# Packed bias operands, twelve early probability tiles through TensorE, bias tables scaled on three engines, two k magnitudes moved

## The chip, the cores and the metric

The kernel is one program on one core of a Trainium2 chip. A core has five engines that run at the same time, each with its own in-order list of instructions: TensorE (PE, matrix products and transposes, with its weight loads shown as PEld), VectorE (DVE), ScalarE (ACT), GpSimd (POOL) and SyncE (SP), which here issues every DMA. The metric is device time in microseconds from the start of the program to its end. Three unprofiled runs of the kernel before took 1791.48, 1793.86 and 1797.2 us; the median, 1793.86 us, is its time. The profile is of one more execution, which took 1798.62 us, with a span of 1796.5 us from the first to the last instruction.

## The reference

An attention layer over 4 batches, 8 heads, 576 positions and head size 64, with a learned additive bias that depends on the two positions only, followed by a layer of eight experts that all see all 2304 rows:

```python
scores = scale * np.matmul(q, k.transpose(0, 1, 3, 2))
x = (log1p(abs(rel)) / log1p(maximum(pos, 1)))[..., None]
h = np.maximum(x @ w1 + b1, 0.0)          # 32 hidden units
scores = scores + (h @ w2).transpose(2, 0, 1)[None]
attn = softmax(scores)
out = np.matmul(attn, v)                  # becomes x of the experts, 2304 x 512
P = exp(x @ w_gate - max), then 8 rounds of row and column normalisation
for e in range(8):
    out += P[:, e:e+1] * (np.maximum(x @ w1[e], 0.0) @ w2[e])
```

## The kernel before

Every operand of a matrix product is split into two fp16 parts, `hi` and `lo`, and three products are added in place of one.

**The order of the work.** In the first part (attention, and the start of expert 0) the Python code does not issue instructions. It records them as nodes with a guessed cost, and `Plan.emit` sorts them: it walks through a modelled time and puts on each engine what is ready first. The order on each engine's list is therefore an outcome of the guessed costs, and any change in the nodes moves other instructions too. All nodes go through one helper line, L202 in the profile, so instructions are told apart by their tiles.

**The bias (blocks 0 to 40).** A host table `xm` holds operands for the 32 hidden units. `bias_front(i)` takes one block `x` of it, loaded by `xm_load` into the tile `xmt` (which lies in `area`), multiplies it by the weights `wa` on PE (into `pv` and the `l` banks) and takes the sign on ACT into `sg` (also in `area`). `bias_back(i)` multiplies the signs by a table on PE (into `s`) and combines the result on DVE. For query tiles 0 and 1 the bias stays on chip in the tables `br[0]` and `br[1]`; tiles 2 and 3 go through a staging tile to `sc_bias` in DRAM and come back per head pair as `bt`; the half tile 4 is kept in `br4`.

**The scale of q and k.** The largest magnitudes of q and k are needed before any score. Sixteen pieces of 128 x 1152 are loaded, q pieces reduced on DVE (`TENSOR_REDUCE`) and k pieces on ACT (`Abs` with a running sum, `some_max`). From them come `mqk`, a broadcast over PE, the scale `s_qk`, and the factor `gbox[0]` by which the tables `br` are then multiplied (`b_scale`, one call per head pair `hp`, two operations each). The same is done for eight pieces of v (`v_max`), which sit in the buffers `bt` and `aT`.

**Attention.** There are 16 units (a batch and a pair of heads), each of 5 steps: two steps of two query tiles for each of the two tile groups `gi` 0 and 1 (one per head `hh`), and one step for the half tile (`gi` 2). Steps 0 to 7 are the `gi` 0 steps of units 0 to 3, run together with the bias blocks; steps 8 to 19 are the `gi` 1 and `gi` 2 steps of these units; after that each unit runs its five. One step is: scores on PE into one of two `s` buffers, bias and maximum on DVE (`sb`), exponential on ACT, `hi` part on ACT and `lo` part on DVE into `ah` (two buffers), a DMA that transposes `ah` into `aT`, and the product with v on PE (`pv`), two steps later.

**Expert 0.** Once the bias blocks have freed `area`, its weights are loaded there (`area<-in_moe_w_dram`), their magnitudes taken, and cut into `hi` and `lo` on ACT and DVE (`w_cut`, the 128 x 1024 operations on `area`). From step 15 on pieces of expert 0 (`l<-xa,area` and the like) are put between the steps on PE. The rest of expert 0 and experts 1 to 7 follow when attention is over.

Of the kernel before, what the change touches and what calls it, by code (L numbers as in the profile page):

```python
# [9 lines left out]
F16 = mybir.dt.float16  # L10
# [3 lines left out]
ALU = mybir.AluOpType  # L14
# [9 lines left out]
N = B * S  # L24
NT = N // P
R = S // 64
EPS = 1e-9
T14 = 2.0**14
TM14 = 2.0**-14
# [233 lines left out]
def attention_sinkhorn_moe(ctx, tc, q, k, v, w1, b1, w2, wg, m1, m2, xm, xm4, xf, sel, out):  # L263
# [141 lines left out]
    with ExitStack() as actx:  # L405
# [64 lines left out]
        def xm_load(i):  # L470
            if i >= NBLK:
                return
            t, s0, n = blk(i)
            x = hidp.tile([P, 4, P], F16, name="xmt", tag="xm", bufs=4)[:, : n // 16, :]
            src = (xm[t] if t < 4 else xm4).rearrange("p (m i) -> p m i", i=P)
            sync.dma_start(out=x, in_=src[:, s0 // 16 : (s0 + n) // 16, :])
            xq[i] = x
# [57 lines left out]
        def bias_front(i):  # L535
            t, s0, n = blk(i)
            W = 8 * n
            xm_load(i + 3)
            if i % 9 == 3 and t < 4:
                xg_load(t + 1)  # L540
            x = xq.pop(i)
            sg = hidp.tile([P, 4, 512], F16, name="sg", tag="sg")
            for g4 in range(4):
                pre = ps_l1() if g4 % 2 else psA.tile([P, 512], F32, name="pre", tag=("pv", "l2")[g4 // 2])
                pe.matmul(pre[:, :W], wa[:, g4], x, start=True, stop=True)
                act.activation(sg[:, g4, :W], pre[:, :W], AF.Sign)
            sgs[i] = sg

# [238 lines left out]
        for n in range(8):  # L787
            for m in (2 * n, 2 * n + 1):
                nm, _, i = qk_order[m]
                some_max(mq8[:, int(nm == "k"), i : i + 1], mxt.pop((nm, i)), nm == "k")  # L790
                if m + 4 < 16:
                    max_load(*qk_order[m + 4])
                elif m + 4 == 16:
                    u_load(0)
                if m + 4 >= 16:
                    max_load("v", v, m - 12)
            bias_step()
            bias_step()
# [20 lines left out]
        def b_scale(hp):  # L819

            for t in range(2):
                x = br[t][:, 2 * hp : 2 * hp + 2, :]
                vec.tensor_scalar(out=x, in0=x, scalar1=gbox[0], scalar2=None, op0=ALU.mult)


        mv8, vbox = sm([P, 8]), []
# [128 lines left out]
        def st_lo(s):  # L955
            n, ah = len(s["sb"]), s["ah"]
            s["aT"] = wrk.tile([P, 9 * n, P], F16, name="aT", tag="aT" if n == 2 else "aT4", bufs=3 if n == 2 else 1)
            for i, sb in enumerate(s["sb"]):
                vec.scalar_tensor_tensor(
                    out=ah[:, i, S:],  # L960
                    in0=sb,
                    scalar=s["st"][:, 3, i : i + 1],
                    in1=ah[:, i, 0:S],
                    op0=ALU.mult,
                    op1=ALU.subtract,
                )
            sync.dma_start_transpose(out=s["aT"], in_=ah.rearrange("p n s -> p (n s)"))

        def attend(u, gi, ss):

# [922 lines left out]
def _constants():  # L1893
    import numpy as np

    pos = np.arange(S)
    rel = (pos[:, None] - pos[None, :]).astype(np.float32)
    x = np.log1p(np.abs(rel)) / np.log1p(np.maximum(pos[:, None].astype(np.float32), np.float32(1.0)))
    x = x.astype(np.float32)
    x4 = x * np.float32(4.0)  # L1900
    hi = x4.astype(np.float16)
    lo = (x4 - hi.astype(np.float32)).astype(np.float16)
    p = np.arange(64)
    half = lambda r: 9 * p + r
    key = np.concatenate([half(c + 4 * r) for c in range(4) for r in range(2)] + [half(8)])
    tiles = [np.concatenate([half(t), half(t + 4)]) for t in range(4)] + [half(8)]
    res, xf = [], []
    for tk in tiles:
        xr = x[np.ix_(tk, key)]
        if len(tk) == P:  # L1910
            xf.append(xr)
        else:
            half_keys = np.concatenate([xr[:, : S // 2], xr[:, S // 2 :]])
            xf.append(np.concatenate([half_keys, 0 * half_keys], axis=1))
        a = np.zeros((4, 32, 36, len(tk)), np.float16)
        for part, src in enumerate((hi, hi, lo, lo)):
            g = src[np.ix_(tk, key)].reshape(len(tk), 36, 4, 4)
            if len(tk) < P:
                g = g.reshape(len(tk), 2, 18, 4, 4).transpose(0, 2, 1, 3, 4).reshape(len(tk), 36, 4, 4)
            a[:, 4 * part : 4 * part + 4] = g.transpose(2, 3, 1, 0)  # L1920
        a[:, 16:18] = 4.0
        res.append(a.reshape(128, -1))
    sel = np.zeros((4, 32, 24), np.float32)
    for g in range(4):
        for r in range(18):
            sel[g, r, r // 4 % 2 if r < 16 else r - 14] = 1.0
            sel[g, r, 8 + 4 * g + np.arange(4)] = [float(r >= 16 or r % 4 == j) for j in range(4)]
        sel[g, :, 4 + g] = 1.0
    return np.stack(res[:4]), res[4], np.stack(xf), sel.reshape(128, 24)


# [26 lines left out]
```

## Time and profile before

| what | value |
|---|---|
| median of three runs | 1793.86 us (1791.48 to 1797.2) |
| profiled execution | 1798.62 us, span 1796.5 us |
| PE busy | 1686.3 us, 94% of the span |
| DVE busy | 1445.9 us, 80% |
| ACT busy | 1086.0 us, 60% |
| POOL busy | 78.7 us, 4% |
| mean granted TensorE clock | 0.979 of full speed |

The shares are means over very different stretches. Attention and the bias fill about the first 530 us; the experts, in which PE is hardly ever idle, fill the rest. The change touches the first 280 us or so, and those have to be read by stretches.

### The profile page before, as it was taken

The numbers are of one execution on the slowest core, as the hardware profiler recorded it, in microseconds if no ns is written. First come the engines' busy times: TensorE is split into PE (matmuls) and PEld (weight loads), VectorE is DVE, ScalarE is ACT, GpSimd is POOL, SyncE is SP. The second block draws the span as 40 slices with busy tenths as digits, with TensorE's granted clock in tenths as the row PEclk, the third lists the DMA queues.
The fourth block names the chain that finished last, engine by engine and source line by source line (L and its number), as shares of the span: only waits on it lengthen the run. The fifth ranks groups of instructions, "written<-read, shape, count | busy, mean of one in ns | idle before, by whom it ended". The sixth has DMA issues, their size and how long they took to land.

```text
span 1796.5 us, 40453 instructions
## 1 busy us (share of the span) xinstructions
PE 1686.3 (94%) x16640; PEld 1375.3 (77%) x16640; DVE 1445.9 (80%) x2627; ACT 1086.0 (60%) x1930; POOL 78.7 (4%) x90
## 2 busy tenths in 40 slices
PE   7787698898989999999999999999999999999998
PEld 4444365555566688888888898889888988898887
DVE  6897888888968798779787887878788878876666
ACT  7887787878856675545564555464555544453443
POOL 0120011222200000000000000000000000000000
PEclk9998699899999999999999999999999999999999
DMA  8879999999993354654475457345645653463321
GB/s 273 256 182 207 224 189 186 190 196 192 199 249 141 104 176 165 219 177 169 174 264 168 173 186 268 135 162 200 235 165 177 222 204 133 157 236 108 104 74 36
DMA packets 305817, 326.55 MB, mean 182 GB/s; under 512 B 191584, under 2 KB 234336, under 8 KB 300640
## 3 DMA queue, kind: packets, MB, share of 16 engines
q1 hardware_dynamic: 305632, 323.97, 60.8%
q8 instruction: 130, 2.13, 0.5%
q14 instruction: 55, 0.45, 0.1%
HBM read 192.18 MB, written 88.08 MB: 156 GB/s over the span
## 4 chain that ended last, share of the span: by engine, by line
PE 76%; DVE 9%; DMA 9%; ACT 3%; issue 2%; SPq 0%; POOL 0%; DVEq 0%; ACTq 0%; POOLq 0%
PE bankA L1581 18%; PE bankA L1601 13%; PE bankE L1601 9%; PE bankE L1581 9%; PE bankB L1601 8%; PE l L202 6%; PE bankB L1581 4%; DMA aT<-ah 4%; PE pv L202 4%; PE s L202 3%; DVE area L202 2%; DVE ah L202 1%; ACT area L202 1%; DVE sb L202 1%; DMA xc<-in_moe_w_dram 1%
## 5 line engine op out<-in xcount | busy, mean ns | idle before, releaser
L1581 PEld LDWEIGHTS <-slot 128*128 128x128 f16 x5040 | 450.7, 98 | 49.7 <-issue 3.8
L1601 PEld LDWEIGHTS <-hA 128*128 128x128 f16 x2268 | 221.8, 98 | 26.7 <-issue 0.6
L202 PEld LDWEIGHTS <-area 128*128 128x128 f16 x2477 | 153.0, 99 | 108.4 <-issue 39.8
L1581 PE MATMUL bankA<-xt,slot 128*128 128x256 f16 (+1 forms) x1680 | 186.1, 262 | 1.6 <-ACT u L1638 1.6
L1581 PE MATMUL bankE<-xt,slot 128*128 128x256 f16 (+1 forms) x1680 | 186.1, 262 | 0.0
L1626 ACT ACTIVATE hA<-c 128x512 f16<-128x512 f32 x189 | 118.1, 627 | 111.0 <-DVE c L1204 110.1
L1601 PEld LDWEIGHTS <-hS 128*128 128x128 f16 x1512 | 147.1, 98 | 23.4 <-ACT hS L1626 3.4
L1601 PEld LDWEIGHTS <-area 128*128 128x128 f16 x1512 | 148.0, 98 | 18.5 <-issue 1.4
L202 DVE SCALAR_TENSOR_TENSOR ah<-sb,st,ah 128x576 f16<-128x576 f32 x144 | 120.2, 861 | 24.8 <-ACT ah L202 24.6
L1204 DVE SCALAR_TENSOR_TENSOR hA<-c,hA 128x512 f16<-128x512 f32 x189 | 127.3, 684 | 14.0 <-ACT hA L1626 11.9
L1685 ACT COPY u<-bankA 128x512 f32<-128x512 f32 (+1 forms) x70 | 37.9, 541 | 160.0 <-PE bankA L1601 159.7
L202 ACT ACTIVATE ah<-sb,st 128x576 f16<-128x576 f32 x144 | 106.2, 770 | 42.9 <-DMA aT<-ah 32.7
L202 PE MATMUL l<-area 128*128 128x512 f16 x413 | 112.0, 390 | 6.2 <-DVE xc L202 1.4
L1638 ACT ACTIVATE u<-bankA 128x512 f32<-128x512 f32 x126 | 75.2, 597 | 67.8 <-PE bankA L1581 63.9
L202 ACT ACTIVATE sb<-sb,st 128x576 f32<-128x576 f32 x144 | 110.4, 769 | 8.4 <-DVE st L202 8.2
L1204 DVE SCALAR_TENSOR_TENSOR acc<-c,fs,acc 128x256 f32<-128x256 f32 x252 | 110.4, 479 | 2.0
L202 PE MATMUL s<-qkT 128*128 128x512 f16 (+3 forms) x560 | 82.0, 296 | 20.7 <-DVE st L202 19.8
L1601 PE MATMUL bankA<-area,hS 128*128 128x256 f16 x756 | 88.6, 273 | 3.3 <-ACT hS L1626 2.7
L1601 PE MATMUL bankA<-area 128*128 128x256 f16 x756 | 88.2, 273 | 1.0 <-ACT u L1685 1.0
L1601 PE MATMUL bankE<-area,hS 128*128 128x256 f16 x756 | 88.6, 273 | 0.6 <-DVE hS L1632 0.6
L1601 PE MATMUL bankA<-area,hA 128*128 128x256 f16 x756 | 88.9, 274 | 0.0
L1601 PE MATMUL bankB<-area 128*128 128x256 f16 x756 | 88.3, 273 | 0.0
(239 smaller groups left out, 3152.5 us busy)
## 6 DMA issues: line engine op xcount, KB each, us to landing
sc_w<-stage SPq DMA_DIRECT2D x84, 512.0 KB, 3.1
acc<-sc_y SPq DMA_DIRECT2D x102, 256.0 KB, 4.3
area<-sc_w SPq DMA_DIRECT2D x48, 512.0 KB, 4.4
sc_y<-acc SPq DMA_DIRECT2D x84, 256.0 KB, 2.3
xt<-sc_t SPq DMA_DIRECT2D x18, 1024.0 KB, 4.8
slot<-sc_w SPq DMA_DIRECT2D x36, 512.0 KB, 5.4
bt<-sc_bias SPq DMA_DIRECT2D x26, 576.0 KB, 4.7
raw<-in_moe_w_dram SPq DMA_DIRECT2D x28, 512.0 KB, 5.1
```

The lines of the kernel that those rows point to most:

```text
L202: self.plan.record(self.name, cost, lambda: fn(*args, **kw), ins, outs, move)
L1204: vec.scalar_tensor_tensor(out=o, in0=x, scalar=s, in1=y, op0=op0, op1=op1)
L1581: pe.matmul(ps[:, jf * w : jf * w + w], t[:, a, c * 512 + f * P : c * 512 + f * P + P], x(xp, c), start=(first and jf == 0 and c == 0 and ...
L1601: pe.matmul(ps[:, j * 256 : j * 256 + 256], h[:, a, fc * w + j * P : fc * w + j * P + P], t[:, wp, fc * 256 : fc * 256 + 256], start=(firs ...
L1626: on_act(0.58, lambda: act.activation(h[:, 0, sl], x, AF.Relu if relu else AF.Copy), [r], wk)
L1638: on_act(0.55, lambda: act.activation(tmp[k], bank[b], f, scale=HS), [b], [k], 0)
L1685: on_act(0.27 * nt, lambda: act.copy(tmp[k][:, :n], bank[b][:, :n]), [b], [k], 0)
```

## The change

Four things are changed. (1) The host table `xm` is packed from four groups of 32 rows, of which 18 were used, to 72 rows; its DMA and the contraction of the `bias_front` product shrink from 128 to 72 rows. (2) For units 0 to 3 the steps with `gi` 2 and the second head's step of `gi` 1 no longer send `ah` through a transposing DMA: PE transposes its nine 128 x 128 blocks per query tile into an `s` buffer, ACT copies five of them to `aT` and DVE four. These are 8 steps with 12 query tiles. (3) `b_scale` stays on DVE for `hp` 0, goes to ACT for `hp` 1 and to POOL for `hp` 2 and 3. (4) The k pieces 2 and 6 are reduced on DVE, the other six on ACT as before.

```diff
-            x = hidp.tile([P, 4, P], F16, name="xmt", tag="xm", bufs=4)[:, : n // 16, :]
+            x = hidp.tile([XR, 4, P], F16, name="xmt", tag="xm", bufs=4)[:, : n // 16, :]
...
-                pe.matmul(pre[:, :W], wa[:, g4], x, start=True, stop=True)
+                pe.matmul(pre[:, :W], wa[:XR, g4], x, start=True, stop=True)
...
-                some_max(mq8[:, int(nm == "k"), i : i + 1], mxt.pop((nm, i)), nm == "k")
+                some_max(mq8[:, int(nm == "k"), i : i + 1], mxt.pop((nm, i)), nm == "k" and i % 4 != 2)
...
-                vec.tensor_scalar(out=x, in0=x, scalar1=gbox[0], scalar2=None, op0=ALU.mult)
+                if hp == 1:
+                    act.activation(x, x, AF.Copy, scale=gbox[0])
+                else:
+                    eng = vec if hp == 0 else pool
+                    eng.tensor_scalar(out=x, in0=x, scalar1=gbox[0], scalar2=None, op0=ALU.mult)
...
-            sync.dma_start_transpose(out=s["aT"], in_=ah.rearrange("p n s -> p (n s)"))
+            u, gi, hh = s["key"]
+            if not (u < NHP and (gi == 2 or (gi, hh) == (1, 1))):
+                sync.dma_start_transpose(out=s["aT"], in_=ah.rearrange("p n s -> p (n s)"))
+                return
+            for i in range(n):
+                ps = ps_s().bitcast(F16)[:, : 9 * P].rearrange("p (r x) -> p r x", x=P)
+                with plan.as_one():
+                    for r in range(9):
+                        pe.transpose(ps[:, r], ah[:, i, r * P : (r + 1) * P], id16)
+                act.copy(s["aT"][:, 9 * i : 9 * i + 5], ps[:, :5])
+                vec.tensor_copy(s["aT"][:, 9 * i + 5 : 9 * i + 9], ps[:, 5:])
...
+XR = 72
-        a = np.zeros((4, 32, 36, len(tk)), np.float16)
+        a = np.zeros((4, XR // 4, 36, len(tk)), np.float16)
```

The order moves in many places. Three matter for what follows.

VectorE, where `mqk` is formed from the sixteen magnitudes (`sms<-sms 128x2`). `bt_121`, `aT_122` and `bt_123` are pieces of v just loaded; `l_0_114 2x1` is the broadcast of `mqk` coming back from PE; the `TENSOR_TENSOR` rows belong to bias blocks. Before:

```order
L202 TENSOR_REDUCE sms<-bt_121 128x1
L202 TENSOR_TENSOR aT_0_117<-s_118,area 128x512
L202 TENSOR_TENSOR br_110<-s_118,aT_0_117 128x2x8x32
L202 TENSOR_REDUCE sms<-sms 128x2
L202 TENSOR_REDUCE sms<-aT_122 128x1
L202 TENSOR_TENSOR aT_0_117<-s_116,area 128x512
L202 TENSOR_REDUCE sms<-bt_123 128x1
L202 TENSOR_TENSOR br_110<-s_116,aT_0_117 128x2x8x32
L202 TENSOR_TENSOR aT_0_117<-s_118,area 128x512
L202 TENSOR_REDUCE sms<-l_0_114 2x1
```

And with the change:

```order
L203 TENSOR_TENSOR aT_0_117<-s_118,area 128x512
L203 TENSOR_TENSOR br_110<-s_118,aT_0_117 128x2x8x32
L203 TENSOR_REDUCE sms<-sms 128x2
L203 TENSOR_REDUCE sms<-bt_121 128x1
L203 TENSOR_TENSOR aT_0_117<-s_116,area 128x512
L203 TENSOR_REDUCE sms<-aT_122 128x1
L203 TENSOR_TENSOR br_110<-s_116,aT_0_117 128x2x8x32
L203 TENSOR_TENSOR aT_0_117<-s_118,area 128x512
L203 TENSOR_REDUCE sms<-l_0_114 2x1
```

The first piece of v now stands behind `mqk`, not ahead of it, and the third (`bt_123`) has gone behind the broadcast.

SyncE's DMA list, where the first stored bias tiles come back (`bt_121` and `bt_123`, one per head of unit 0). Before:

```order
L202 DMA sc_bias<-area 128x8x64
L202 DMA bt_121<-sc_bias 128x1152
L202 DMA br_111<-area 64x4x128 x2
L202 DMA_TRANSPOSE aT_122<-ah_144 128x18x128
L202 DMA br_111<-area 64x4x128 x2
L202 DMA bt_123<-sc_bias 128x1152
L202 DMA br_111<-area 64x4x128 x2
L202 DMA area<-in_moe_w_dram 128x2x512
```

And with the change:

```order
L203 DMA sc_bias<-area 128x8x64
L203 DMA nat_128<-in_q_dram 64x2x256 x2
L203 DMA nat_128<-in_q_dram 128x64
L203 DMA bt_121<-sc_bias 128x1152
L203 DMA bt_123<-sc_bias 128x1152
L203 DMA br_111<-area 64x4x128 x2
L203 DMA_TRANSPOSE aT_122<-ah_144 128x18x128
L203 DMA br_111<-area 64x4x128 x4
L203 DMA area<-in_moe_w_dram 128x2x512
```

The second load has moved from behind a transposing DMA and two pairs of `br_111` transfers to the place right behind the first.

VectorE again, where expert 0's weights are cut (`area<-area,sms 128x1024`) between steps 9 to 11. Before:

```order
L202 ISA sb_133,st_139<-s_118,bt_123,sms 128x576
L202 ISA st_139 128x1
L202 SCALAR_TENSOR_TENSOR area<-area,sms 128x1024
L202 ISA sb_134,st_143<-s_116,br_111,sms 128x576
L202 ISA st_143 128x1
L202 TENSOR_SCALAR st_139<-st_139 128x2
```

And with the change:

```order
L203 ISA sb_133,st_139<-s_118,bt_123,sms 128x576
L203 ISA st_139 128x1
L203 COPY aT_0_117<-s_116 128x512
L203 SCALAR_TENSOR_TENSOR xa<-pv_112,xa 128x256
L203 SCALAR_TENSOR_TENSOR area<-area,sms 128x1024
L203 ISA sb_134,st_143<-s_118,br_111,sms 128x576
L203 ISA st_143 128x1
L203 TENSOR_SCALAR st_139<-st_139 128x2
```

One of the twelve copies out of an `s` buffer (step 10's tile) now stands ahead of the second cut; of the twelve, two stand ahead of the first weight magnitudes that wait for the load, four between these and the last cut, and six behind it. On POOL's list the two `TENSOR_SCALAR` of `br[0]` stand ahead of unit 0's two copies `qkT<-qkT`, and those of `br[1]` between these and unit 1's.

## Rows read from the trace of the kernel before

**Rows 1.** Page, part 4: the chain that ended last, by engine.

```profile
PE 76%; DVE 9%; DMA 9%; ACT 3%; issue 2%; SPq 0%; POOL 0%; DVEq 0%; ACTq 0%; POOLq 0%
```

**Rows 2.** Windows: stretch, length, busy us (x instructions) of each engine, clock, DMA.

```profile
0.00:62.00 62.00, 48.66 (x661) 29.45 (x662) 44.56 (x83) 47.45 (x92) 1.51 (x10) 1.00 0.85 282
62.00:137.00 75.00, 59.34 (x805) 36.34 (x804) 71.87 (x139) 64.22 (x124) 17.88 (x17) 0.98 0.78 198
137.00:183.00 46.00, 30.26 (x386) 18.70 (x384) 33.26 (x76) 32.95 (x70) 1.61 (x3) 0.89 0.93 221
183.00:219.00 36.00, 21.46 (x194) 13.09 (x196) 33.64 (x74) 26.55 (x46) 1.62 (x3) 0.70 0.97 217
219.00:240.00 21.00, 21.00 (x192) 14.22 (x189) 16.24 (x39) 15.80 (x33) 4.36 (x5) 0.86 0.70 144
240.00:277.00 37.00, 35.52 (x368) 22.89 (x368) 31.99 (x72) 31.18 (x64) 7.57 (x7) 1.00 1.00 209
```

**Rows 3.** VectorE in order of time: start, length, operation [idle before it, releaser].

```profile
51.74 1.35 DVE L202 TENSOR_REDUCE sms<-bt 128x1 f32<-128x1152 f32 x1 [2.64 <-DMA bt<-in_v_dram]
54.34 0.16 DVE L202 TENSOR_REDUCE sms<-sms 128x2 f32<-128x16 f32 x1
```

**Rows 4.** Groups by line and form, 0 to 520 us: q and k magnitudes.

```profile
L202 DVE TENSOR_REDUCE sms<-area 128x1 f32<-128x1152 f32 x8 | 10.8, 1346 | 0.3 <-DMA area<-in_q_dram 0.2
L202 ACT ACTIVATE area<-area 128x1152 f32<-128x1152 f32 x8 | 10.3, 1290 | 1.1 <-DMA area<-in_k_dram 1.1
```

**Rows 5.** DMA issues, 0 to 60 us: count, KB each, median us to landing.

```profile
area<-const_xm_dram SPq DMA_DIRECT2D x21, 128.0 KB, 4.7
```

**Rows 6.** Tile br on VectorE, 55 to 140 us: ns min/median/max.

```profile
L202 DVE TENSOR_SCALAR br<-br,sms x8: 791/808/1776, 62.3 to 120.0; 128x1152 f32<-128x1152 f32 x8
```

**Rows 7.** Groups, 0 to 520 us: POOL's nearest operation.

```profile
L202 POOL COPY qkT<-qkT 64x1152 f16<-64x1152 f16 x28 | 33.3, 1190 | 282.2 <-ACT qkT L202 281.4
```

**Rows 8.** Timeline of all engines: a table operation beside POOL's copies.

```profile
66.77 1.78 DVE L202 TENSOR_SCALAR br<-br,sms 128x1152 f32<-128x1152 f32 x1
66.79 2.76 POOL L202 COPY qkT<-qkT 64x1152 f16<-64x1152 f16 x2 [64.68 <-ACT qkT L202]
```

**Rows 9.** SP's list in order of time: the returns of the bias tiles.

```profile
149.92 0.33 SPq L202 DMA_DIRECT2D bt<-sc_bias  x1
152.59 3.74 SPq L202 DMA_TRANSPOSE aT<-ah  x1
157.70 0.61 SPq L202 DMA_DIRECT2D bt<-sc_bias  x1
```

**Rows 10.** Waits, 0 to 176 us: in total, times, longest.

```profile
DVE sb L202 <- DMA bt<-sc_bias: 2.9, 1, 2.9
```

**Rows 11.** Groups, 0 to 520 us: copies of fp16 blocks out of PSUM.

```profile
L202 DVE COPY qkT<-l 128x1024 f16<-128x1024 f16 x14 | 9.6, 687 | 4.6 <-PE l L202 4.1 <-ACT qkT L202 0.4
L202 ACT COPY qkT<-l 128x1024 f16<-128x1024 f16 x14 | 14.0, 999 | 3.7 <-PE l L202 3.7
```

**Rows 12.** PE in order of time: equal groups at two clocks, and eight transposes.

```profile
220.50 2.77 PE L202 MATMUL l<-area 128*128 128x512 f16 x6
236.58 1.46 PE L202 MATMUL l<-area 128*128 128x512 f16 x6
238.85 0.61 PE L202 MATMUL l<-id,qk 128*128 128x128 f16 x8
```

**Rows 13.** DMA, 260 to 500 us: all packets, and the transposes issued.

```profile
DMA packets 118904, 46.42 MB, mean 193 GB/s; under 512 B 110301, under 2 KB 114653, under 8 KB 118877
aT<-ah SPq DMA_TRANSPOSE x50, 5.1
```

**Rows 14.** Waits, 183 to 277 us.

```profile
PE s L202 <- DVE st L202: 7.8, 6, 2.1
ACT ah L202 <- DMA aT<-ah: 3.1, 3, 1.5
PE pv L202 <- DVE xa L202: 2.4, 2, 2.0
```

More of the change, by code (lines that the diff above doesn't have):

```diff
@@ L1921, in _constants @@
         a[:, 16:18] = 4.0
-        res.append(a.reshape(128, -1))
-    sel = np.zeros((4, 32, 24), np.float32)
+        res.append(a.reshape(XR, -1))
+    sel = np.zeros((128, 24), np.float32)
     for g in range(4):
         for r in range(18):
[L1926 to L1929, printed above, removed]
+            sel[18 * g + r, r // 4 % 2 if r < 16 else r - 14] = 1.0
+            sel[18 * g + r, 8 + 4 * g + np.arange(4)] = [float(r >= 16 or r % 4 == j) for j in range(4)]
+        sel[32 * g : 32 * g + 32, 4 + g] = 1.0
+    return np.stack(res[:4]), res[4], np.stack(xf), sel
 _CN = ("xm", "xm4", "xf", "sel")
```

## The prediction

> **What bounds the kernel now.** I read the chain that ended last first. PE holds 76% of it, DVE 9% and the DMA 9% [rows 1], but the change touches only the first 280 us, where attention and the bias run, so the next view was a table of stretches [rows 2]. There the bound moves. From 0 to 62 us, up to the scale of q and k, no engine is full: ACT has 47.45 us of work, DVE 44.56, and the DMA is 0.85 busy. From 62 to 137 us, bias blocks beside steps 0 to 7, DVE works 71.87 of 75 us: it is the bound. From 137 to 183 us all engines idle a third of the time and the DMA is 0.93 busy: the last bias tiles go out and come back, then expert 0's weights arrive. From 183 to 219 us, while these are cut, DVE is busy 33.64 of 36 us, PE only 21.46. From 219 to 240 us PE is busy throughout, with pieces of expert 0 that had to wait for the cut, and the DMA falls to 0.70. To 277 us PE (35.52 of 37) and the DMA (1.00) are both full.
>
> A step finished earlier anywhere there carries through, since every later step runs behind it at the same pace; the question is what each edit is worth in its own stretch.
>
> **Step 1, the scale of q and k (0 to 62 us).** On DVE's list the piece of v ahead of `mqk` waited 2.64 us for its load, and `mqk` followed at 54.34 [rows 3]. That piece now stands behind `mqk` and the third piece of v behind the broadcast. Between `mqk` and the returning broadcast there are two pieces as before, so what leaves the way is the wait and one reduction, 2.64 + 1.35 = 4.0 us. The two k pieces that DVE takes over cost 2 x 1.35 us [rows 4], ahead of `mqk`; they lie in DVE's 17.4 us of idle time in this stretch, and ACT loses 2 x 1.29 us of work with them. If DVE's idle time did not cover them, 1.3 us would remain; if ACT's relief came on top, it would be 6.6. I take -4.0.
>
> The narrower `xm` blocks: 21 loads of 128 KB [rows 5] lose 56 KB each, 1.2 MB, which at the 282 GB/s of the stretch [rows 2] is 4.2 us of DMA time. No row shows a wait of that size for them, so I take 0, and the 4.2 as the other end. PE's products keep their columns, so I take 0 there; only the rows summed over shrink, and no row has a matmul whose time fell with them.
>
> The Trainium skill, SBUF — State Buffer, section "Can I just issue two DMAs to hit both halves?", speaks against this edit: only one transfer across all 128 partitions reaches all 16 ports. By DMA: Bandwidth & Descriptors, "Why a DMA increments its semaphore by 16 and not by 1", 72 rows would be spread over 12 of the 16 engines, six rows each in place of eight; then the 4.2 us would be at most 2.4. No row here shows how a load is spread over engines, and neither figure is in the sum.
>
> **Step 2, the tables (62 to 137 us).** Eight scaling operations on DVE have a median of 0.81 us and one of 1.78 [rows 6]. Two stay. The six that leave are worth 5 x 0.81 + 1.78 = 5.8 us of the engine that bounds the stretch; the piece of v that came in behind the broadcast gives back 1.35. What POOL's four operations cost has no row. The nearest is its copy of 64 x 1152 fp16, 1.19 us [rows 7]; fp32 on 128 rows may cost that or twice that. Beside such copies one table operation on DVE took 1.78 in place of 0.81 us during 2.76 us of POOL [rows 8]: 0.35 us lost for each us of POOL. Four operations of 1.4 us (half of 2.76) are 5.6 us of POOL and cost DVE 1.9 us; the ends are 0 and, at 2.4 us each with two thirds of it lost, 6.4. Sum of the step -5.8 + 1.35 + 1.9 = -2.6 us, ends -4.5 and +1.9. POOL's table operations stand ahead of and between the `qkT` copies that the first scores need, but POOL idles 64.68 us before the first pair [rows 8] and is busy 17.88 of 75 us in the stretch [rows 2], so I take nothing for that. ACT's two operations, 1.29 us each by the same 128 x 1152 shape [rows 4], lie in its 10.8 idle us.
>
> By the Trainium skill, SBUF — State Buffer, "Who interferes with whom", DVE and POOL share a port pair as an exclusive lock and the loser waits for a whole instruction. By that DVE would lose up to all 5.6 us of POOL's time, and the step would be +1.2 us. The row shows a loss of a third of it, so the trace bears the lock out only in part, and I stay with the row.
>
> **Step 3, the returning bias tiles (137 to 183 us).** The second load of `bt` was issued at 157.70 us, 7.8 us behind the first, with a transposing DMA that held SP's list for 3.74 us between them [rows 9]. DVE waited 2.9 us for it [rows 10], and the steps and DMAs behind DVE with it. The load now stands right behind the first. I take the wait, -2.9 us; the ends are 0, if the loads of weights set the time in any case, and the 7.8 us of the issue.
>
> **Step 4, the cut (183 to 219 us).** A copy of 128 x 1024 fp16 out of PSUM takes DVE 0.69 and ACT 1.00 us [rows 11]. Of four blocks and five I take 0.4 and 0.65 us (ends 0.34 and 0.69; 0.62 and 1.0). Four of the twelve DVE copies stand between the arrival of the weights and the last cut, in the stretch that DVE bounds: +1.6 us, ends 1.4 and 2.8. ACT's lie in its 9.4 idle us.
>
> **Step 5, PE (219 to 277 us).** Eight transposes took 0.61 us [rows 12], nine take 0.69, twelve tiles 8.2 us. The first six lie in PE's 14.5 idle us before 219; the last six, 4.1 us, come when PE is full. Against it stands the clock: from 219 to 240 us the granted clock was 0.86 on the mean, after a stretch in which PE was busy 21.46 of 36 us [rows 2], and the same six matmuls took 2.77 us at the lower level and 1.46 later [rows 12]. If PE, with more to do ahead, held the upper level, 21 x 0.14 = 2.9 us would come back; I take half, so +2.7 us, ends +1.2 and +4.1.
>
> **Step 6, the DMAs that go.** From 260 to 500 us 50 issues carry 90 tiles of 295 KB, 26.5 of 46.42 MB [rows 13]; the other 19.9 MB at 282 GB/s take 71 us, which leaves about 1.8 us of a DMA stretch that is nearly full for a tile. Twelve tiles are 22 us. But in 183 to 240 us DVE and then PE are full, and waits of ACT for `ah` to be read are 3.1 us in three [rows 14]. I take a third, -1.0; the ends are 0 and half of the 22.
>
> **Sum.** -4.0 - 2.6 - 2.9 + 1.6 + 2.7 - 1.0 = -6.2 us. The profiled execution took 1798.62 us, which makes 1792.4; it lies 4.8 us above the median of the runs, so against that median I forecast 1793.86 - 6.2, about 1787.6 us. The later steps are reordered too, by a few places, for which I take 0.
>
> **Rivals.**
> *PE waits in its own list: slower.* The eight DMAs waited on SP's list; their transposes stand on PE's, and scores and pieces of expert 0 behind each wait until DVE has made the low half and until an `s` buffer has been copied out. Waits of PE for DVE of just this kind reach 2.0 and 2.1 us [rows 14]. At 2.1 us for each of eight steps, 16.8 us, the sum is +10.6, 1804 us. It turns slower than the bound from 1.5 us per step on. Against it: PE idles 14.5 us before 219 us anyway.
> *The DMA was the bound.* It is 0.97 busy from 183 to 219 and 1.00 from 240 us on [rows 2]. If half of the 22 us came out, in place of 1.0, the time would be 1778. Against it: 0.70 in between, with PE full.
> *Nothing arrives.* Steps 1 and 2 end in the stretch from 137 us, where the DMA is 0.93 busy and stores of bias tiles set the pace; without their 6.6 us the sum is +0.4, 1794 us. For it: all engines idle there.
>
> **How the numbers follow.** The forecast has 0.47 (it spreads over 1781 to 1792: 0.35 faster, 0.12 within), the DMA 0.17, all faster, nothing arriving 0.18 (0.14 within, 0.04 slower), PE waiting 0.18 (0.14 slower, 0.04 within). Three runs cannot tell less than 0.3%, 5.4 us, from no change; so faster 0.52, same 0.30, slower 0.18. For the range I leave out the outer parts of the first and last rivals: 1776 to 1799 us; the forecast's own range is 1781 to 1792.
>
> **What would show it.** In the changed profile: `mqk` near 50 us and not behind a wait for v (step 1); DVE still over 93% busy up to the point where the first `sc_bias` tiles are complete, reached 6 to 7 us earlier, and POOL's table operations of 1.2 to 2.4 us (step 2); no wait of `sb` for `bt` (step 3); the last cut 9 us earlier, less 1.6 (step 4); a granted clock near 1.0 behind it, and no wait of PE for `ah` above 1 us (step 5, first rival); fewer waits of ACT for `ah` (step 6). The prediction is wrong if PE's transposes wait, if the weights arrive no earlier than 182 us, or if the steps behind step 20 run at another pace.

## The result and the profile after

The changed kernel is slower: 1802.86 us (median of 11 runs) against 1794.23, ratio 1.0052, 95% interval 1.0042 to 1.0062. That is 9 us where I forecast a gain of 6. The profiled execution took 1803.46 us, near its median; that of the kernel before lay 4.4 us above its own. So times are compared below by ratios, and profiles only for what stands where.

The stretches after answer to [rows 2]:

```profile
0.00:62.00 62.00, 47.55 (x659) 29.48 (x660) 47.10 (x88) 46.71 (x90) 2.49 (x11) 0.99 0.82 257
62.00:137.00 75.00, 63.41 (x768) 38.90 (x768) 70.53 (x123) 58.41 (x112) 27.66 (x18) 0.82 0.68 180
137.00:183.00 46.00, 33.62 (x438) 20.77 (x435) 36.31 (x78) 38.05 (x79) 4.22 (x6) 0.89 0.89 211
183.00:219.00 36.00, 23.78 (x227) 15.11 (x227) 32.09 (x75) 26.40 (x48) 0.00 (x0) 0.75 0.73 182
219.00:240.00 21.00, 19.24 (x185) 13.66 (x184) 16.62 (x36) 16.11 (x34) 4.87 (x5) 0.77 0.37 76
240.00:277.00 37.00, 33.40 (x318) 20.75 (x317) 29.25 (x68) 28.41 (x58) 5.13 (x5) 0.95 0.72 159
```

From 62 to 137 us DVE is as busy as before, 70.53 in place of 71.87 us, but does 123 instructions in place of 139. POOL has 27.66 us in place of 17.88. The granted clock of that stretch fell from 0.98 to 0.82; that is no measure of the loss, since in the fastest version below (edits 1 and 4 alone) it was 0.86 there. What the two do there is in the timeline of POOL and then of DVE, which answers to [rows 8]:

```profile
61.00 7.26 POOL L203 TENSOR_SCALAR br<-br,sms 128x1152 f32<-128x1152 f32 x2 [58.91 <-DVE sms L203]
71.48 3.39 POOL L203 COPY qkT<-qkT 64x1152 f16<-64x1152 f16 x2 [3.22 <-ACT qkT L203]
74.97 6.87 POOL L203 TENSOR_SCALAR br<-br,sms 128x1152 f32<-128x1152 f32 x2
81.90 2.93 POOL L203 COPY qkT<-qkT 64x1152 f16<-64x1152 f16 x2
...
60.94 0.82 DVE L203 TENSOR_SCALAR br<-br,sms 128x1152 f32<-128x1152 f32 x1
61.67 6.96 DVE L203 SCALAR_TENSOR_TENSOR qk<-nat,sms,qk 128x576 f16<-128x576 f32 x2
68.56 0.51 DVE L203 TENSOR_SCALAR area<-area,sms 128x576 f32<-128x576 f32 x1
...
75.65 3.13 DVE L203 TENSOR_SCALAR br<-br,sms 128x1152 f32<-128x1152 f32 x1
78.70 0.67 DVE L203 COPY qkT<-l 128x1024 f16<-128x1024 f16 x1
79.29 0.80 DVE L203 CUSTOM_DVE_ANT_0 sb<-s,br,sms 128x576 f32<-128x576 f32 x1
```

POOL's four table operations took 14.1 us, 3.5 each. The first pair of q and k pieces, which the first scores wait for, took DVE 6.96 us, and ends 0.4 us behind POOL's pair; a table operation took 3.13 us in place of 0.81 and ends 0.4 us behind POOL's third. The copy out of PSUM (0.67) and the `sb` operation (0.80) run beside POOL at their usual length. In the table of tile `br`, the first `sb` moves from 72.9 us (first row, before) to 79.3 (second row, after):

```profile
L202 DVE CUSTOM_DVE_ANT_0 sb<-s,br,sms x80: 794/808/818, 72.9 to 507.6; 128x576 f32<-128x576 f32 x80
```

```profile
L203 DVE CUSTOM_DVE_ANT_0 sb<-s,br,sms x80: 792/809/819, 79.3 to 512.4; 128x576 f32<-128x576 f32 x80
```

Later, the PE steps brought waits of their own. These are seven rows of the waits from 183 to 277 us, which answer to [rows 14]:

```profile
ACT aT L203 <- DVE aT L203: 9.3, 5, 4.3
PE s L203 <- DVE st L203: 4.0, 6, 2.1
PE pv L203 <- DVE xa L203: 3.9, 1, 3.9
ACT ah L203 <- DMA aT<-ah: 3.2, 3, 1.4
PE s L203 <- DVE aT L203: 3.0, 2, 2.3
PEld L203 <- DVE ah L203: 2.9, 3, 1.4
PE s L203 <- DVE ah L203: 2.3, 2, 1.2
```

The last cut of a weight starts at 221.33 us; before it was 215.59. From DVE's timelines, before and after:

```profile
215.59 1.27 DVE L202 SCALAR_TENSOR_TENSOR area<-area,sms 128x1024 f16<-128x1024 f32 x1
221.33 1.28 DVE L203 SCALAR_TENSOR_TENSOR area<-area,sms 128x1024 f16<-128x1024 f32 x1
```

### The profile page after: what moved, and what is told of

It reads as the page before. It is cut to its first block, busy times and chain, and to the rows that moved or that the text cites. A ratio compares the mean times of both kernels' runs of the same rounds, so it can differ in the third digit from the quotient of the medians.

```text
span 1801.8 us, 40682 instructions
## 1 busy us (share of the span) xinstructions
PE 1698.3 (94%) x16748; PEld 1385.0 (77%) x16748; DVE 1457.8 (81%) x2635; ACT 1092.3 (61%) x1940; POOL 92.5 (5%) x94
## 4 chain that ended last, share of the span: by engine, by line
PE 76%; DMA 9%; DVE 9%; issue 3%; ACT 3%; SPq 1%; DVEq 0%; ACTq 0%
PE bankA L1596 17%; PE bankA L1616 13%; PE bankE L1596 9%; PE bankE L1616 8%; PE bankB L1616 8%; PE l L203 5%; PE bankB L1596 4%; DMA aT<-ah 4%; PE s L203 4%; PE pv L203 3%; PE bankA L386 2%; DVE sb L203 2%; DVE ah L203 1%; DVE area L203 1%; PE bankB L367 1%
## 5 line engine op out<-in xcount | busy, mean ns | idle before, releaser
L1616 PEld LDWEIGHTS <-hA 128*128 128x128 f16 x2268 | 221.6, 98 | 28.7 <-ACT hA L1641 1.1
L203 PEld LDWEIGHTS <-area 128*128 128x128 f16 (+1 forms) x2477 | 156.0, 100 | 106.4 <-issue 35.2
L1616 PEld LDWEIGHTS <-area 128*128 128x128 f16 x1512 | 147.9, 98 | 19.0 <-issue 1.9
L203 PE MATMUL l<-area 128*128 128x512 f16 (+1 forms) x413 | 110.1, 388 | 7.3 <-ACT area L203 2.5
L203 PE MATMUL s<-qkT 128*128 128x512 f16 (+3 forms) x560 | 81.8, 296 | 20.5 <-DVE st L203 17.6
L1616 PE MATMUL bankE<-area,hA 128*128 128x256 f16 x756 | 88.8, 273 | 1.2 <-ACT hA L1641 0.8
```

The costliest lines, as they stand in the source:

```text
L203: self.plan.record(self.name, cost, lambda: fn(*args, **kw), ins, outs, move)
L1616: pe.matmul(ps[:, j * 256 : j * 256 + 256], h[:, a, fc * w + j * P : fc * w + j * P + P], t[:, wp, fc * 256 : fc * 256 + 256], start=(firs ...
```

## The experiments

The theories for the first four: A, POOL's table operations hold DVE up; B, the PE transposes make the loss (the rival "PE waits in its own list"). Ratios are to the kernel before on the same chip, with their 95% intervals; 0.001 is 1.8 us.

**No POOL scaling in the changed kernel.**

```diff
-                    eng = vec if hp == 0 else pool
-                    eng.tensor_scalar(out=x, in0=x, scalar1=gbox[0], ...)
+                    vec.tensor_scalar(out=x, in0=x, scalar1=gbox[0], ...)
```

> The changed kernel with head pairs 2 and 3 of the bias tables scaled on VectorE again; ScalarE keeps head pair 1, all other edits stay. Theory A (GpSimd's four table operations, 3.2 to 3.8 us each in the changed profile, hold VectorE up: a pair of q and k operations took 6.96 us there in place of 2.4, one table operation 3.13 in place of 0.8, and the first scores came 7 us later): those pairs are back at 1.6 to 2.4 us, the first transposing DMA is issued near 94 us again in place of 101.0, and the time falls by 6 to 10 us, to about 1795. Theory B (the PE transposes make the loss): the time stays within 3 us of the changed kernel's 1803.

Measured: 1.0037 (1.0022 to 1.0052). The first `sb` is back at 71.3 us, but only about 2.7 of the 9 us came back, and the two intervals (this one and the changed kernel's) overlap. By the time this is what B expected, not A: the place of the first scores was restored, and most of the loss stayed.

**POOL scaling alone, in the kernel before.**

```diff
-                vec.tensor_scalar(out=x, in0=x, scalar1=gbox[0], ...)
+                if hp == 1:
+                    act.activation(x, x, AF.Copy, scale=gbox[0])
+                else:
+                    eng = vec if hp == 0 else pool
+                    eng.tensor_scalar(out=x, in0=x, scalar1=gbox[0], ...)
```

> The kernel before with the third edit alone (tables scaled on VectorE, ScalarE and GpSimd). Theory A: slower than before by 6 to 10 us, about 1802, with the first transposing DMA near 101 us. Theory B: within 3 us of before, or faster by the 2.6 us of step 2 of the prediction.

Measured: 1.0052 (1.0038 to 1.0066), 9 us, as A said; the first `sb` stands at 84.1 us.

**No PE transposes in the changed kernel.**

```diff
-            if not (u < NHP and (gi == 2 or (gi, hh) == (1, 1))):
-                sync.dma_start_transpose(out=s["aT"], ...)
-                return
-            for i in range(n):
...
-                        pe.transpose(ps[:, r], ah[:, i, r * P : (r + 1) * P], id16)
-                act.copy(s["aT"][:, 9 * i : 9 * i + 5], ps[:, :5])
-                vec.tensor_copy(s["aT"][:, 9 * i + 5 : 9 * i + 9], ps[:, 5:])
+            sync.dma_start_transpose(out=s["aT"], ...)
```

> The changed kernel with all tiles transposed by DMA again. Theory A: the loss stands before the first transposed tile, so the time stays within 4 us of the changed kernel's 1803; by steps 4 to 6 of the prediction (+1.6 +2.7 -1.0) it falls by 3.3. Theory B (waits of PE in its own list, +16.8 us): the time falls by 8 to 17 us, below 1795.

Measured: 1.0011 (0.9997 to 1.0025). The twelve tiles are worth 7.4 us of the loss, just short of B's 8, although the first `sb` stands at 78.7 us.

**PE transposes alone, in the kernel before:** the lines that the last diff takes out, put in.

```diff
-            sync.dma_start_transpose(out=s["aT"], ...)
+            if not (u < NHP and (gi == 2 or (gi, hh) == (1, 1))):
...
+                        pe.transpose(ps[:, r], ah[:, i, r * P : (r + 1) * P], id16)
...
```

> The kernel before with the second edit alone (12 tiles transposed on TensorE). Theory A: within 4 us of before; by the prediction's steps 4 to 6, +3.3 us, 1797. Theory B: slower by 8 us or more, 1802 and above.

Measured: 1.0061 (1.0046 to 1.0075), 11 us: B again. Both parts cost, and each alone about as much as the whole change, so their costs don't simply add; the remaining edits may give something back.

**Neither of them:** edits 1 and 4, and head pair 1 on ACT; in the changed kernel

```diff
-                    eng = vec if hp == 0 else pool
-                    eng.tensor_scalar(out=x, in0=x, scalar1=gbox[0], ...)
+                    vec.tensor_scalar(out=x, in0=x, scalar1=gbox[0], ...)
...
-            if not (u < NHP and (gi == 2 or (gi, hh) == (1, 1))):
...
```

> The changed kernel with neither GpSimd's scaling (VectorE has head pairs 0, 2 and 3, ScalarE 1) nor PE transposes: the first and fourth edit and ScalarE's part of the third. If the parts add up (changed kernel without PE transposes 2 us slower than before, GpSimd's scaling alone 9 us), this is faster than before by 4 to 8 us, ratio 0.9955 to 0.998, and the scale of q and k is ready near 57 us in place of 61. If the loss of GpSimd's scaling was only an order of the later steps that any edit upsets, it lies within 3 us of before.

Measured: 0.9992 (0.9981 to 1.0003). No loss, but less gain than adding up said. The scale was ready 2.8 us earlier (the reciprocal of `s_qk` at 58.56 us, 61.31 before) and the first `sb` was not (73.2 and 72.9).

**72 rows alone.**

```diff
+XR = 72
...
-            x = hidp.tile([P, 4, P], F16, name="xmt", tag="xm", bufs=4)...
+            x = hidp.tile([XR, 4, P], F16, name="xmt", tag="xm", bufs=4)...
...
```

> The kernel before with the first edit alone (72 rows in the bias operands). Prediction's step 1: the narrower loads are worth 0, the other end 4.2 us. A gain near 4 us says that the loads set the first 62 us; within 2 us of before, that they don't; a loss, that 72 rows are worse spread over the DMA engines than 128.

Measured: 0.9999 (0.9987 to 1.0012): nothing, as taken.

**The twelve tiles in halves.**

```diff
-            if not (u < NHP and (gi == 2 or (gi, hh) == (1, 1))):
+            if not (u < 2 and (gi == 2 or (gi, hh) == (1, 1))):
```

and with `2 <= u < NHP` for the late half.

> The kernel before with the first six of the twelve tiles alone on TensorE (units 0 and 1, at 179 to 209 us in the profile with all twelve). Theory C (TensorE has no free time from expert 0's first piece to the end, so a transposed tile costs its 0.68 us there and nothing ahead of it): within 2 us of before. Theory D (each PE step costs a wait in the lists of TensorE, ScalarE and VectorE wherever it stands): half of the loss with all twelve, +5 us.

Measured: 1.0005 (0.9996 to 1.0014): the first six cost nothing that can be told.

> The kernel before with the last six of the twelve tiles alone on TensorE (units 2 and 3, at 216 to 246 us in the profile with all twelve). Theory C: +4.1 us at least, and all of what twelve cost. Theory D: +5 us, half of what twelve cost.

Measured: 1.0038 (1.0024 to 1.0051), 7 us, nearly all in the late half, and more than 4.1. C and not D, so far.

**POOL's operations later.** Into the kernel without both, POOL's scaling comes back with a factor that depends on the state of an earlier step.

```diff
+            gs = gbox[0]
+            if hp > 1:
+                gs = sm([P, 1])
+                vec.scalar_tensor_tensor(out=gs, in0=steps[2 * hp - 4]["st"][:, 3, 0:1],
+                    scalar=0.0, in1=gbox[0], op0=ALU.mult, op1=ALU.add)
...
-                    vec.tensor_scalar(out=x, in0=x, scalar1=gbox[0], ...)
+                    eng = vec if hp == 0 else pool
+                    eng.tensor_scalar(out=x, in0=x, scalar1=gs, ...)
```

> The kernel with the first and fourth edit and ScalarE's part of the third (within 0.1% of before when timed), with head pairs 2 and 3 of the tables on GpSimd again, but made to wait for the first and third step of attention, so that they run near 95 and 115 us, where VectorE scaled them before, and not on top of the first q and k pieces. If GpSimd's operations only cost where they meet the pieces that the first scores wait for: first scores near 73 us again and within 3 us of before, or faster by the VectorE work saved, 3 us. If they cost VectorE their whole length wherever they stand: 14 us of GpSimd against 3.2 us saved, slower than before by 4 to 10 us.

Measured: 1.0007 (0.9995 to 1.0019), 2.7 us above the kernel that it was built on. The first `sb` was on time (72.2 us), and DVE lost its time at the new place: in the timelines of POOL and DVE one piece of 0.5 us took 3.38,

```profile
89.28 6.57 POOL L203 TENSOR_SCALAR br<-br,sms 128x1152 f32<-128x1152 f32 x2 [1.13 <-DVE sms L203]
89.41 3.38 DVE L203 TENSOR_SCALAR area<-area,sms 128x576 f32<-128x576 f32 x1
```

so the holding up is not tied to the first pieces. The time lies where the expectation put it if only the first pieces counted, but the run without PE transposes speaks against that reason: it has the same four operations on top of the first pieces, its first `sb` at 78.7 us in place of 72.2, and its ratio of 1.0011 can't be told from this 1.0007. The ninth `sb` starts at 120.0 us there and at 120.1 us here. Moving the operations away from the first scores gained nothing that can be seen.

**POOL on a tile that nothing reads.**

```diff
+        idle = wrk.tile([P, DM], F32, name="ys", tag="ys")
+        pool.memset(idle, 0.0)
...
+                if hp > 1:
+                    pool.tensor_scalar(out=idle, in0=idle, scalar1=gbox[0], ...)
```

> The kernel before, all tables on VectorE, plus four operations of GpSimd (128 x 512, fp32) on a tile that nothing reads, started by the same scale; no other engine's list changes. They take some 6 us, as the first pair of table operations does in the changed kernel. If the two engines hold each other up: the first pair of q and k operations takes about 7 us in place of 1.54, the first scores come 5 us later, and the time grows by 4 to 6 us. If the loss of GpSimd's scaling came from the order of the lists alone: within 2 us of before.

Measured: 1.0008 (0.9993 to 1.0023): a miss for A. POOL and DVE:

```profile
63.07 8.53 POOL L202 TENSOR_SCALAR ys<-ys,sms 128x512 f32<-128x512 f32 x4 [47.21 <-DVE sms L202]
...
63.66 1.98 DVE L202 SCALAR_TENSOR_TENSOR qk<-nat,sms,qk 128x576 f16<-128x576 f32 x2
...
67.79 0.80 DVE L202 TENSOR_SCALAR br<-br,sms 128x1152 f32<-128x1152 f32 x1
```

Here the pair of pieces took 1.98 us. So either the shape matters, or the loss was one of order; the run of ones below decides.

**The late transposes twice over.**

```diff
-                    for r in range(9):
+                    for r in [*range(9), *range(9)]:
```

> The kernel before with the last six of the twelve tiles on TensorE, and each transposed twice over into the same place. Theory C (from expert 0's first piece on TensorE's own work is the time): 54 more transposes, 4.1 us more than the 1.0038 measured with one pass, so 1.006. If it is the waits and the copies behind the transposes that cost: within 1.5 us of one pass.

Measured: 1.0015 (1.0003 to 1.0026). 54 transposes more did not add 4 us to the loss of the late half; C falls as a rule for the time.

**The k magnitudes alone.**

```diff
-                some_max(mq8[...], mxt.pop((nm, i)), nm == "k")
+                some_max(mq8[...], mxt.pop((nm, i)), nm == "k" and i % 4 != 2)
```

> The kernel before with the fourth edit alone (two k magnitudes on VectorE). Prediction's step 1: the scale of q and k is ready 3 to 4 us earlier and the time falls by 4 us. If the first scores wait for something else (granted clock, q and k transposes, loads), the scale is ready earlier, the first scores are not, and the time stays within 2 us of before.

Measured: 0.9988 (0.9975 to 1.0001). The magnitudes were reduced at 52.04 us (54.34 before, [rows 3]) with no wait for v ahead, the reciprocal stands at 59.46, the first `sb` at 73.2. The scale comes earlier, as step 1 said, and the first scores do not.

**Idle transposes.** All tiles by DMA, and the late six besides into a place that nothing reads.

```diff
             sync.dma_start_transpose(out=s["aT"], ...)
+            if 2 <= u < NHP and (gi == 2 or (gi, hh) == (1, 1)):
+                for i in range(n):
+                    ps = ps_s().bitcast(F16)[:, : 9 * P].rearrange("p (r x) -> p r x", x=P)
...
+                            pe.transpose(ps[:, r], ah[:, i, r * P : (r + 1) * P], id16)
```

> The kernel before, all tiles transposed by DMA, and besides the last six of the twelve transposed once on TensorE into a place that nothing reads: the same 54 transposes as in the run with the late tiles alone, without the copies and with the DMAs kept. If TensorE's work itself is what the late tiles cost: the stretch behind expert 0's first pieces, 26.0 us before and 29.6 with the late tiles, is again 29 to 30 us, and the time grows by 4 us, ratio 1.002. If it is the copies and the waits for them: 26 us there, and within 1.5 us of before.

Measured: 0.9995 (0.9983 to 1.0006). PE is busy throughout from 232 to 258 us, in the kernel before (first row) and here (second):

```profile
232.00:258.00 26.00, 26.00 (x265) 15.84 (x264) 21.68 (x53) 21.01 (x44) 3.03 (x4) 1.00 0.98 200
232.00:258.00 26.00, 25.98 (x263) 16.19 (x262) 20.28 (x50) 20.17 (x42) 2.29 (x2) 1.00 0.96 185
```

The stretch of the expectation (from the start of the 37th `sb` to that of the 49th) took 27.9 us: the work shows there, and not in the time.

**POOL multiplies by one.**

```diff
+        one = sm([P, 1])
+        vec.tensor_scalar(out=one, in0=gbox[0], scalar1=0.0, scalar2=1.0, op0=ALU.mult, op1=ALU.add)
+        def b_one(hp):
+            for t in range(2):
+                x = br[t][:, 2 * hp : 2 * hp + 2, :]
+                pool.tensor_scalar(out=x, in0=x, scalar1=one[:, 0:1], ...)
...
-        hook(0, lambda: [b_scale(1), u_load(2), ...
+        hook(0, lambda: [b_scale(1), b_one(2), b_one(3), u_load(2), ...
```

> The kernel before, all tables scaled on VectorE, and GpSimd multiplies head pairs 2 and 3 by one, in place, with the four operations of 128 x 1152 that the change gives it, started by the same scale. If such an operation holds VectorE's two-operand pieces up for its whole length: the first pair of q and k operations takes about 7 us, the first scores come 6 us or more late, and the time grows by 8 to 14 us (as with GpSimd's scaling alone, 9, and with no work saved on VectorE). If they share as with the tile that nothing reads (pair 1.98 us, time within 0.1%): within 3 us of before, and the loss of GpSimd's scaling was one of order.

Measured: 1.0063 (1.0050 to 1.0076), 11 us. POOL and DVE in order of time:

```profile
62.06 7.19 POOL L202 TENSOR_SCALAR br<-br,sms 128x1152 f32<-128x1152 f32 x2 [59.96 <-DVE sms L202]
72.57 3.58 POOL L202 TENSOR_SCALAR br<-br,sms 128x1152 f32<-128x1152 f32 x1
79.17 3.20 POOL L202 TENSOR_SCALAR br<-br,sms 128x1152 f32<-128x1152 f32 x1
...
61.92 4.26 DVE L202 SCALAR_TENSOR_TENSOR qk<-nat,sms,qk 128x576 f16<-128x576 f32 x2
73.00 3.75 DVE L202 TENSOR_SCALAR br<-br,sms 128x1152 f32<-128x1152 f32 x1
79.47 3.52 DVE L202 TENSOR_SCALAR br<-br,sms 128x1152 f32<-128x1152 f32 x1
```

The first q piece began ahead of POOL; the second, and two table operations, last as long as POOL's. With no work taken from DVE, POOL's four operations cost 11 us. A holds for operations of this shape.

**Edits 1 and 4 alone:** 72 rows and the k magnitudes, tables on DVE, tiles by DMA; in the changed kernel

```diff
-                if hp == 1:
-                    act.activation(x, x, AF.Copy, scale=gbox[0])
...
+                vec.tensor_scalar(out=x, in0=x, scalar1=gbox[0], ...)
...
-            if not (u < NHP and (gi == 2 or (gi, hh) == (1, 1))):
...
```

> The first and the fourth edit alone: 72 rows and two k magnitudes on VectorE, all tables on VectorE, all tiles by DMA. The best that the parts promise: k magnitudes alone measured 0.9988, 72 rows 0.9999. If they add, 0.9985 to 0.999, 1 to 3 us faster than before and 11 us faster than the changed kernel; if the scale's earlier time is given back at the first scores, within 0.1% of before.

Measured: 0.9981 (0.9971 to 0.9990), 1788.83 us: faster than the kernel before by 3.4 us and than the changed one by 13. It is the version that the parts point to.

**ACT's part of the tables alone.**

```diff
-                vec.tensor_scalar(out=x, in0=x, scalar1=gbox[0], ...)
+                if hp == 1:
+                    act.activation(x, x, AF.Copy, scale=gbox[0])
+                else:
+                    vec.tensor_scalar(out=x, in0=x, scalar1=gbox[0], ...)
```

> The kernel before with head pair 1 of the tables scaled on ScalarE alone. The prediction took ScalarE's two operations to lie in its idle time and VectorE to save 0.81 and 1.78 us: 0 to 2 us faster. If ScalarE's operations stand ahead of its q and k pieces and delay the first scores: 1 to 2 us slower.

Measured: 1.0001 (0.9992 to 1.0009): nothing.

**The late half with ACT's copy alone, and the late half again.** The first of the two, against the late half:

```diff
-                act.copy(s["aT"][:, 9 * i : 9 * i + 5], ps[:, :5])
-                vec.tensor_copy(s["aT"][:, 9 * i + 5 : 9 * i + 9], ps[:, 5:])
+                act.copy(s["aT"][:, 9 * i : 9 * i + 9], ps)
```

> The kernel before with the late six tiles on TensorE, and each copied out of PSUM by ScalarE alone (9 blocks) in place of ScalarE and VectorE. If the loss with the late six (1.0038) is the waits between the two copies and VectorE's share of them: back to within 0.1% of before. If it lies in the places that TensorE's list gives the steps there: 1.003 or more again.

Measured: 1.0032 (1.0019 to 1.0044). Neither DVE's share nor the wait between the two copies is the cost.

> The late six tiles alone once more, word for word, beside the run above on one chip, since doubling the transposes gave less (1.0015) than one pass (1.0038) on another day. If the late six truly cost, 1.003 to 1.005 again. If the first measurement was high, 1.001 to 1.002, as with the doubled ones, and the loss of all twelve (1.0061) lies in the two halves together.

Measured: 1.0034 (1.0021 to 1.0046): the loss of the late half is there again, 6 us.

## Why the prediction was wrong

**Step 2 failed, and most plainly.** Its term was -2.6 us with ends of -4.5 and +1.9; on top of edits 1 and 4 the tables cost 5.4 us (1.0011 against 0.9981). ACT's part alone is worth 0 in the kernel before (on edits 1 and 4 it took 2 us, 0.9992 against 0.9981, with intervals that overlap), so most of the loss is POOL's. Two numbers were wrong. "1.4 us each" came from a copy of 64 rows in fp16; POOL's operations took 3.2 to 3.8, beyond my upper end of 2.4. And "0.35 us lost for each us of POOL" counted one of the two DVE pieces that were stretched beside POOL's copies in [rows 8]. The copies ran from 66.79 to 69.55 us, and the next pair of DVE began inside them and took 2.42 us; undisturbed, at 63.08 us in the same profile, such a pair takes 1.54:

```profile
68.46 2.42 DVE L202 SCALAR_TENSOR_TENSOR qk<-nat,sms,qk 128x576 f16<-128x576 f32 x2
```

So DVE lost 0.97 + 0.88 = 1.85 us there, two thirds of 2.76, which I had only as the upper end. In the changed profile it lost 5.4 us in the first pair, 2.3 in a table operation and 0.6 in the piece at 80.76 us, 8.4 of 14.1 us. With that the term is -5.8 + 1.35 + 8.4 = +4.0.

DVE's lost time is also enough for what POOL's operations cost in every run that had them. I count each DVE piece beside them against its length without them (0.81 us for `qk`, table and `ah` pieces, 0.51 for `area`), and take off the 4 x 0.81 = 3.2 us that DVE no longer works where POOL scales:

| POOL's operations | DVE lost | less what it saves | measured |
|---|---|---|---|
| in the changed kernel (taken out) | 8.4 us | 5.2 | 2.7 |
| on edits 1 and 4 with ACT's part | 8.4 | 5.2 | 3.4 |
| the same, later | 7.3 | 4.1 | 2.7 |
| scaling alone, in the kernel before | 11.5 | 8.3 | 9 |
| multiplying by one | 10.3 | 10.3 | 11 |
| on the unread tile | 0.8 | 0.8 | 1.4 |

The measured values have 2 to 3 us of uncertainty on either side, and all six sums lie within it. No further cost for late first scores is needed: with them late or on time the measured costs can't be told apart.

The Trainium skill, SBUF — State Buffer, "Who interferes with whom", was the better guide, and I set it aside for the row. It says that the loser of the shared port pair waits for a whole instruction, that DVE operations with two SBUF inputs and `tensor_scalar` in its two-port modes can be the loser, and that those with one SBUF input outside these modes cannot. By that, the term with 14.1 us of POOL in place of 5.6 would have been up to -5.8 + 1.35 + 14.1 = +9.65 us, an estimate of its upper end. The trace agrees on which pieces lose: those that stretched are of the first kinds, and the copy out of PSUM and `sb` were not stretched. In the run on an unread tile of 128 x 512 it does not agree: DVE's operation at 67.79 us took its 0.80 us inside POOL's of 1.83 us, which had begun at 67.22.

**Step 5 and its rival.** Steps 4 to 6 made +3.3 us of the twelve tiles; they cost 7.4 us (undone) to 11 us (alone), and of the halves the late one has nearly all. That the first six cost nothing was right. The last six were priced at 4.1 us of PE work, and this reason is wrong: they cost 6 to 7, the same transposes without the copies cost nothing, and doubling them added nothing. The clock half of 2.9 us did not come: 0.77 from 219 to 240 us, 0.86 before. But that isn't the cause either: in the profiles of the late half alone, of its repetition and of ACT's copy the clock there was 0.99, 0.94 and 1.00, and the loss stood all the same.

The rival "PE waits in its own list" named 1804 us, and 1802.86 came; that is luck. It put 2.1 us of wait on each of eight steps, 16.8 in all; PE's waits for `ah` and `aT` are 2.9 + 2.3 + 3.0 = 8.2 us from 183 to 277, other waits became shorter (for `st` 4.0 in place of 7.8), and by [rows 2] and the rows that answer to them PE idled 17.6 of these 94 us in place of 16.0. In the late half alone PE, the first figure behind the length, did not wait in the stretch from the 37th `sb` to the 49th:

```profile
230.00:259.70 29.70, 29.70 (x318) 19.32 (x317) 23.84 (x59) 24.51 (x52) 2.29 (x2) 1.00 0.66 142
```

That stretch was 26.0 us before; it took 28.7 to 31.0 us in all seven profiles with the late six and at most 26.6 in the others, but 27.9 with the idle transposes, which cost no time. So the longer stretch can't simply be added to the time, and what in the late half costs 6 us stays open: not PE's work alone, not the clock there, not DVE's copy, not the wait of ACT for it. Left are that the values pass through a copy at all, and hold an `s` buffer until it is done, the DMAs that go, and the order that the lists take with both.

**Step 4** had the right sign in another size: the last cut came 5.7 us later than before, not 7.4 earlier; with the PE tiles alone it came 3.5 us later (219.10), against +1.6.

**Step 6:** the DMA was freed, 0.73 busy from 183 and 0.37 from 219 us in place of 0.97 and 0.70, and no gain was seen. That speaks against "The DMA was the bound" too.

**Step 1** held in sign and size, not in its way. In the changed profile `mqk` is reduced at 51.71 us and not behind a long wait for v, and edits 1 and 4 alone give 3.4 us (by the interval 1.8 to 5.2) against 4.0. But the scale was 2.4 us earlier in that run (58.92 and 61.31), and the first `sb` at 72.7 us was not. Where the 3.4 us come from isn't shown; 72 rows alone are worth 0, as taken, and the k magnitudes alone 2 us, within an interval that reaches to 0.

**Step 3:** the wait of `sb` for `bt` is gone, as said, and no time was seen to come of it: the loads of weights were issued from 163.0 to 178.7 us, before from 159.7 to 176.1. By itself it wasn't tried.

Step by step from the kernel before, edits 1 and 4 make -3.4 us, the tables on top of them +5.4, the tiles on top of that +7.4 (1.0052 against 1.0011). Such a chain gives the measured 9.3 by construction and tests nothing. Each alone in the kernel before, the three come to -3.4 + 9 + 11 = +17. That DVE lost 8.4 us beside POOL in the changed kernel and 11.5 with the scaling alone makes 3 us of the difference; the rest isn't explained. "Nothing arrives", at 1794 us, missed that edits 1 and 4 gain and that the other two lose.

## What to carry to other kernels

Price work that moves to GpSimd by an operation of its own shape and type, and look at which VectorE pieces will stand beside it, all of them and not only the nearest: those with two SBUF operands, and `tensor_scalar` from SBUF to SBUF, lost up to the whole length of GpSimd's operation, those that read PSUM nothing. Where VectorE bounds a stretch, what it lost counted here as much away from the first step of the chain as ahead of it. A full engine is no proof that more work on it costs, and a full DMA none that taking work from it pays: try the part alone, and its halves.

## What had not been expected of the hardware

GpSimd took 3.2 to 3.8 us for a 128 x 1152 fp32 `tensor_scalar` that VectorE does in 0.81 and ScalarE in 1.25. How much VectorE loses was not the same in all runs: with 128 x 1152 it lost 7.3 to 11.5 of some 14 us, with 128 x 512 only 0.8 of 8.5 us. There GpSimd took 1.8 to 2.5 us for one operation; by length alone I would estimate 3.2 x 512 / 1152 = 1.4 us, so it may have lost in its turn. No run has it undisturbed, and why the shapes differ is not known.

PE was busy all of 26 us from 232 to 258 us in the kernel before, and 54 transposes more, about 4 us, left the time where it was (0.9995). PE had 26 idle us (243 less 216.7) from 277 to 520 us, in which such a delay could be made up; no run shows that it was.
